# Four low weight parts: a negated copy on ScalarE and an adding transfer instead of a subtract on VectorE

## The chip, the cores and the metric

The kernel runs on one core of a Trainium2 chip. The metric is the device time of one execution in microseconds (us). Three runs of the kernel before gave 973.69, 974.58 and 974.63 us; their median is 974.58.

In the profile PE is the engine of the matrix products, DVE the vector engine, ACT the scalar engine, POOL the GpSimd engine and SP the engine that here issues nearly all transfers.

## The reference

```
mag = sqrt(a_re^2 + a_im^2);  a = (a_re + i a_im) * min(mag, 0.999) / (mag + 1e-6)
for t in range(768):                       # per batch (4) and head (8), state is 48 x 48, complex
    S = a[t] * S + k[t] (outer) v[t]
    y[t] = q[t] @ real(S)
x = y as 3072 tokens x 384
x = (h - tanh(h)) @ w_out1   with h = x @ w_in1      # 384 -> 2048 -> 384
x = (relu(h)^2) @ w_out2     with h = x @ w_in2
```

The weights come as 64-bit floats. The products have to be nearly as good as float32.

## The kernel before

The recurrence is cut into six chunks of 128 time steps for each of four batch entries, which makes 24 units (`unit`). Tokens are worked in six groups of 512; the two feed-forward layers are worked in 16 blocks m of 128 hidden columns for each group. A block is nine products into `h` (`g1`), an activation (`act_parts`), and nine products into three accumulators `acc` (`g2`), two blocks later. There are nine because every operand is held as a high part, rounded to the format fp32r that PE multiplies at full pace, and a low part, the rest: for each of three slices of the contraction, high times high, high times low and low times high are added up.

The weights of a block are 128 x 768 values, `w_in` and `w_out` side by side. They are loaded as 64-bit words into `st` (768 KB, two buffers), joined to float32 by three DVE instructions into `cv` (two buffers, tag "cv", `conv_do`, lines 214 to 239), and split by `conv_split` (line 270) with `split_w` (line 276): ACT writes the high part `wh`, DVE subtracts it from `cv` and writes the low part `wl`. A `cv` buffer is free again when both have read it, and the block after next then writes it. `wh` and `wl` have a place of their own for each m in `wpool`. The places of m = 4 to 15 are first used by tiles of the units 1 to 3 (`early`), all of which are done with when these weights are written.

The order of the work: a list START starts the first units and blocks of weights, then `block_step(t)` is called for each block; t = 0 and 1 are the two halves of m = 0, t = 2 is m = 1, and so on to t = 16, which is m = 15. At block t, `conv_upto` brings the joining of weights up to `JOINS` blocks ahead. So the split of m = 4 is issued at the block of m = 2, that of m = 5 at m = 3, those of m = 6 and 7 at m = 4, and that of m = 14 at m = 11. On PE and SP each engine's order is then as written (`Turn`, and `chain`); on DVE and ACT it is pinned from t = 17 and t = 15 on, and before that, in all of the stretch that the change touches, the framework's list scheduler chooses among what is ready by its own durations. Each engine works its queue in order: an instruction whose wait is not over holds up all behind it.

POOL writes constants at the start and then has nothing to do until it splits tokens for the second layer. All transfers but one, an output at the very end, go out on SP's queue.

Of the kernel before, what the change touches and what calls it, by code (L numbers as in the profile page):

```python
# [12 lines left out]
F32 = mybir.dt.float32  # L13
# [4 lines left out]
ALU = mybir.AluOpType  # L18
# [18 lines left out]
1x 0pU 2s0 2m0 0st 3e0 3s0 2e1 4sq J 4ln 1st 3s1 3pU 3m0 2s1 2m1 3st 3m1 2px 3px 2pU 2st B 2x 3x  # L37
"""
AHEAD = (1, 1, 1, 2, 2, 3, 4, 5, 5, 6, 7, 8, 8, 8, 9, 9, 10, 11, 11, 11, 12, 13, 13, 15, 15, 15, 16, 16)
JOINS = (4, 2, 3, 3, 4, 3, 2, 2, 2, 2, 3, 4, 3, 2, 2, 3, 4)  # L40


@with_exitstack
def kernel(
# [9 lines left out]
    nc = tc.nc  # L54
# [47 lines left out]
    def clear_strips():  # L102
# [11 lines left out]
        out=maskab[:, 0], in_=maskab[:, 0], compare_op=ALU.is_ge, fill=0.0, base=0,  # L114
        pattern=[[1, P]], channel_multiplier=-1,
    )
    for g in range(4):
        m = maskab[32 * g:32 * g + 32, 1]
        nc.gpsimd.affine_select(
            out=m, in_=m, compare_op=ALU.is_ge, fill=0.0, base=-32 * (3 - g),  # L120
# [6 lines left out]
        out=past, in_=past, compare_op=ALU.is_ge, fill=0.0, base=-1,  # L127
# [41 lines left out]
    act_e = Turn(nc.scalar, "act")  # L169
# [44 lines left out]
    def conv_do(layer, m):  # L214
        st = stg.pop((layer, m))
        lo, hi = words(st)
        if layer == 0:
            t = spool.tile([P, n2], I32, tag="cv", name=f"cv{layer}_{m}", bufs=2)
        else:
            t = cpool[0].tile([P, n2], I32, tag="jw", name=f"jw{m}", bufs=2)  # L220
        tf = t.bitcast(F32)
        with ExitStack() as es:
            if (layer, m) == (0, 1):
                es.enter_context(tc.issue_after(chain["gate"]))
            dve.tensor_scalar(
                t, hi, 3, 0x3FFFFFFF, op0=ALU.logical_shift_left, op1=ALU.bitwise_and
            )
        yield
        dve.scalar_tensor_tensor(
            t, lo, 29, t, op0=ALU.logical_shift_right, op1=ALU.bitwise_or  # L230
        )
        yield
        dve.scalar_tensor_tensor(
            t, hi, -0x40000000, t, op0=ALU.bitwise_and, op1=ALU.bitwise_or
        )
        if layer == 0 and 0 < m < NM - 1:
            conv_split(layer, m, tf)
        else:
            joined[m] = tf
# [30 lines left out]
    def conv_split(layer, m, tf):  # L270
        wh = wpool.tile([P, n2], F32R, tag=f"wh{m}", name=f"wh{layer}_{m}")
        wl = wpool.tile([P, n2], F32R, tag=f"wl{m}", name=f"wl{layer}_{m}")
        split_w(wh, wl, tf)
        wts[layer, m] = (wh, wl)

    def split_w(wh, wl, tf):
        act_e.copy(wh, tf)
        dve.tensor_tensor(wl, tf, wh.bitcast(F32), op=ALU.subtract)
# [755 lines left out]
    def conv_upto(k):  # L1034
        while cdone[0] < k:
            conv_tick()
# [20 lines left out]
    s_first = 3 - (NST - 1)  # L1057
    pos = AHEAD
    assert len(pos) == NM - s_first
# [59 lines left out]
    def block_step(t):  # L1119
# [3 lines left out]
        if t < NB0:  # L1123
            conv_upto(min(NM, blocks[t][2] + JOINS[t]))
            steps = ahead[t]
# [5 lines left out]
        if t < NB:  # L1131
# [8 lines left out]
            if t == NB0 - 2:  # L1140
                conv_split(0, NM - 1, joined.pop(NM - 1))
# [34 lines left out]
        if t >= NATT + LAG:  # L1176
            for _ in range(2):
                if cdone[0] < len(cq):
                    conv_tick()
            m2 = cur["split"]  # L1180
            if m2 in joined and t >= NATT + LAG + m2:
                conv_split(1, m2, joined.pop(m2))
                cur["split"] += 1
# [122 lines left out]
```

## Time and profile before

| | us |
|---|---|
| median of three runs | 974.58 |
| the profiled execution | 973.18 |
| its span, first to last instruction | 971.1 |
| PE busy | 950.1 (98%) |
| ACT busy | 635.2 (65%) |
| DVE busy | 540.7 (56%) |
| POOL busy | 19.5 (2%) |

The page gives busy times of the whole span; its line of 40 slices shows that DVE and ACT are at nine or ten tenths in the first five or six slices (some 24 us each) and far below that later, and that PE's granted clock is 0.9 or more in every slice. A busy PE is not a PE at its full pace, because products are pipelined: a product of 512 columns is shown as 0.39 us, while the next starts after 0.23 us.

### The profile page before, as it was taken

The numbers are of one execution on the slowest core, as the hardware profiler recorded it, in microseconds if no ns is written. First come the engines' busy times: TensorE is split into PE (matmuls) and PEld (weight loads), VectorE is DVE, ScalarE is ACT, GpSimd is POOL, SyncE is SP. The second block draws the span as 40 slices with busy tenths as digits, with TensorE's granted clock in tenths as the row PEclk, the third lists the DMA queues.
The fourth block names the chain that finished last, engine by engine and source line by source line (L and its number), as shares of the span: only waits on it lengthen the run. The fifth ranks groups of instructions, "written<-read, shape, count | busy, mean of one in ns | idle before, by whom it ended". The sixth has DMA issues, their size and how long they took to land.

```text
span 971.1 us, 18373 instructions
## 1 busy us (share of the span) xinstructions
PE 950.1 (98%) x7437; PEld 786.2 (81%) x7437; DVE 540.7 (56%) x902; ACT 635.2 (65%) x1110; POOL 19.5 (2%) x43
## 2 busy tenths in 40 slices
PE   5999999999999999999999999999999999999997
PEld 2888788888888888888888888888888888888886
DVE  7999987666666666665548993132322322322111
ACT  8879978777777777786534455465666665555442
POOL 2000000000000000000000010000000000000000
PEclk9999999999999999999999999999999999999999
DMA  8345413222322232221136552063444353330001
GB/s 315 131 148 165 151 45 92 59 58 64 101 68 70 63 92 64 69 75 42 58 126 224 176 169 79 1 195 104 163 143 140 93 176 113 130 97 31 33 1 34
DMA packets 53481, 100.99 MB, mean 104 GB/s; under 512 B 19712, under 2 KB 29200, under 8 KB 53392
## 3 DMA queue, kind: packets, MB, share of 16 engines
q1 hardware_dynamic: 53248, 99.65, 32.4%
q8 instruction: 59, 0.97, 0.4%
q14 instruction: 30, 0.25, 0.1%
q10 hardware_dynamic: 144, 0.13, 0.0%
HBM read 87.08 MB, written 9.46 MB: 99 GB/s over the span
## 4 chain that ended last, share of the span: by engine, by line
PE 89%; ACT 5%; DVE 5%; DMA 1%; issue 1%; ACTq 0%
PE h L161 39%; PE acc L161 38%; PE px L161 3%; PE strips L161 2%; PE pk L161 1%; PE pq L161 1%; ACT ab L161 1%; PE pU L161 1%; DVE cv L161 1%; ACT L161 1%; PE pu L161 1%; PE sc L161 1%; PE pc L161 1%; ACT fg L161 1%; ACT ee L161 1%
## 5 line engine op out<-in xcount | busy, mean ns | idle before, releaser
L161 DVE TENSOR_TENSOR gl<-t,gh 128x512 fp32r<-128x512 f32 (+1 forms) x193 | 132.2, 685 | 215.4 <-ACT gh L161 215.1
L161 ACT ACTIVATE t<-h 128x512 f32<-128x512 f32 (+1 forms) x193 | 114.6, 594 | 194.0 <-PE h L161 191.4
L161 PE MATMUL acc<-gh,wh 128*128 128x512 f32 (+1 forms) x579 | 229.3, 396 | 0.0
L161 PE MATMUL h<-xh,wh 128*128 128x512 f32 (+1 forms) x579 | 228.0, 394 | 0.6 <-DVE t L161 0.4
L161 PE MATMUL h<-xh,wl 128*128 128x512 f32 (+1 forms) x579 | 225.1, 389 | 0.0
L161 PE MATMUL acc<-gl,wh 128*128 128x512 f32 (+1 forms) x579 | 225.0, 389 | 0.0
L161 PE MATMUL acc<-gh,wl 128*128 128x512 f32 (+1 forms) x579 | 224.8, 388 | 0.0
L161 PE MATMUL h<-xl,wh 128*128 128x512 f32 (+1 forms) x579 | 224.0, 390 | 0.0
L161 ACT CAST gh<-t 128x512 fp32r<-128x512 f32 (+1 forms) x191 | 118.0, 618 | 87.0 <-PE acc L161 46.2
L161 PEld LDWEIGHTS h<-xh,wh 128*128 128x128 f32 x579 | 108.7, 188 | 26.6 <-issue 3.2
L161 PEld LDWEIGHTS h<-xh,wl 128*128 128x128 f32 x579 | 108.7, 188 | 22.7
L161 PEld LDWEIGHTS acc<-gh,wl 128*128 128x128 f32 x579 | 108.7, 188 | 22.6
L161 PEld LDWEIGHTS acc<-gl,wh 128*128 128x128 f32 x579 | 108.9, 188 | 21.9 <-DVE gl L161 0.2
L161 PEld LDWEIGHTS acc<-gh,wh 128*128 128x128 f32 x579 | 108.8, 188 | 21.6
L161 PEld LDWEIGHTS h<-xl,wh 128*128 128x128 f32 x579 | 108.7, 188 | 21.1
L161 DVE TENSOR_TENSOR t<-h,t 128x512 f32<-128x512 f32 (+1 forms) x97 | 65.8, 679 | 59.8 <-ACT t L161 59.7
L161 ACT ACT_TABLE_LOAD x63 | 80.8, 1283 | 1.7 <-PEq L1288 0.8
L161 ACT ACTIVATE t<-t 128x512 f32<-128x512 f32 x96 | 60.3, 628 | 1.6
L161 DVE TENSOR_TENSOR wmin<-wmin,cz 128x768 bf16<-128x768 bf16 x32 | 17.8, 557 | 57.4 <-ACT cz L161 57.4
L161 DVE TENSOR_TENSOR wm<-strips,maskab 128x512 f32<-128x512 f32 x32 | 21.8, 690 | 29.1 <-PE strips L161 29.1
L161 DVE SCALAR_TENSOR_TENSOR jw<-st,jw 128x768 int32<-128x768 int32 x32 | 30.4, 950 | 0.2
L161 DVE SCALAR_TENSOR_TENSOR cv<-st,cv 128x768 int32<-128x768 int32 x32 | 30.4, 949 | 0.2
(141 smaller groups left out, 977.7 us busy)
## 6 DMA issues: line engine op xcount, KB each, us to landing
st<-in_w_dram SPq DMA_DIRECT2D x32, 768.0 KB
sr<-in_w_dram SPq DMA_DIRECT2D x32, 768.0 KB
ri<-in_ri_dram SPq DMA_DIRECT2D x24, 384.0 KB
qk<-in_qk_dram SPq DMA_DIRECT2D x24, 384.0 KB
vz<-in_v_dram SPq DMA_DIRECT2D x16, 384.0 KB
x2d<-x2t SPq DMA_DIRECT2D x18, 256.0 KB
xf<-x2d SPq DMA_DIRECT2D x6, 768.0 KB
ss<-in_ri_dram SPq DMA_DIRECT2D x12, 384.0 KB
```

The source lines that it names most:

```text
L161: r = op(*a, **kw)
```

## The change

For m = 4, 5, 6 and 14 of the first layer, the low part is made in another way: ACT writes minus the high part into `wl`, and a transfer from POOL's queue adds `cv` to it in place. The other twelve blocks of the first layer and all of the second keep the subtract on DVE.

```diff
+BY_DMA = (4, 5, 6, 14)
 JOINS = (4, 2, 3, 3, 4, 3, 2, 2, 2, 2, 3, 4, 3, 2, 2, 3, 4)
...
         wh = wpool.tile([P, n2], F32R, tag=f"wh{m}", name=f"wh{layer}_{m}")
         wl = wpool.tile([P, n2], F32R, tag=f"wl{m}", name=f"wl{layer}_{m}")
-        split_w(wh, wl, tf)
+        if layer == 0 and m in BY_DMA:
+            act_e.copy(wh, tf)
+            act_e.mul(wl, wh.bitcast(F32), -1.0)
+            nc.gpsimd.dma_start(out=wl, in_=tf, accum_op=ALU.add)
+        else:
+            split_w(wh, wl, tf)
         wts[layer, m] = (wh, wl)
```

## Rows read from the trace of the kernel before

**Rows 1.** Busy time by stretch: stretch, length, PE, PEld, DVE, ACT, POOL, clock, DMA, GB/s.
```profile
50.00:60.00 10.00, 10.00 (x116) 8.78 (x105) 9.84 (x18) 6.34 (x15) 0.00 (x0) 1.00 0.42 151
60.00:70.00 10.00, 9.81 (x45) 7.78 (x44) 9.93 (x16) 9.03 (x15) 0.00 (x0) 1.00 0.49 158
...
520.00:960.00 440.00, 440.00 (x1943) 364.06 (x1942) 164.91 (x242) 243.59 (x428) 11.73 (x15) 1.00 0.33 107
```

**Rows 2.** PE's longest group of waits, 50 to 150 us: who, whom, us, times, longest.
```profile
PE pk L161 <- DVE kn L161: 1.0, 2, 0.7
```

**Rows 3.** Writes of `wh` up to 140 us: count, ns least/median/most, first, last.
```profile
L161 ACT CAST wh<-cv x16: 818/832/890, 18.3 to 131.1; 128x768 fp32r<-128x768 f32 x16
```

**Rows 4.** POOL in order of time, its first instruction after the start: start us, us, instruction, wait.
```profile
504.84 0.62 POOL L361 TENSOR_SCALAR xh<-xf 128x512 fp32r<-128x512 f32 x1 [498.41 <-DVE gl L161]
```

**Rows 5.** SP in order of time, the load of 384 KB before DVE's wait.
```profile
133.78 0.35 SPq L161 DMA_DIRECT2D qk<-in_qk_dram  x1
```

**Rows 6.** Busy time by stretch, columns as in the first group, while a load of `st` runs.
```profile
51.00:52.00 1.00, 1.00 (x11) 0.95 (x9) 1.00 (x3) 0.69 (x3) 0.00 (x0) 1.00 1.00 418
```

**Rows 7.** DVE in order of time, 49 to 69 us, around weights and activations.
```profile
49.71 0.95 DVE L161 TENSOR_TENSOR wl<-cv,wh 128x768 fp32r<-128x768 f32 x1
...
53.58 0.55 DVE L161 TENSOR_SCALAR cv<-st 128x768 int32<-128x768 int32 x1
...
54.79 0.96 DVE L161 TENSOR_TENSOR wl<-cv,wh 128x768 fp32r<-128x768 f32 x1 [0.16 <-ACT wh L161]
55.67 0.42 DVE L161 TENSOR_TENSOR gl<-t,gh 128x256 fp32r<-128x256 f32 x1
...
59.61 0.55 DVE L161 TENSOR_SCALAR cv<-st 128x768 int32<-128x768 int32 x1
60.08 0.95 DVE L161 TENSOR_TENSOR wl<-cv,wh 128x768 fp32r<-128x768 f32 x1
...
66.68 0.55 DVE L161 TENSOR_SCALAR cv<-st 128x768 int32<-128x768 int32 x1
...
68.14 0.68 DVE L161 TENSOR_TENSOR t<-h,t 128x512 f32<-128x512 f32 x1
```

**Rows 8.** PE in order of time, places that wait for what the change moves.
```profile
56.14 0.39 PE L161 MATMUL acc<-gl,wh 128*128 128x256 f32 x1
...
68.88 0.50 PE L161 MATMUL h<-xh,wh 128*128 128x512 f32 x1 [0.19 <-DVE t L161]
...
100.79 0.39 PE L161 MATMUL h<-xh,wl 128*128 128x512 f32 x1
101.27 0.61 PE L161 MATMUL pk<-ident,kn 128*96 128x128 f32 x4
...
132.12 0.40 PE L161 MATMUL h<-xh,wl 128*128 128x512 f32 x1
...
133.90 0.61 PE L161 MATMUL pk<-ident,kn 128*96 128x128 f32 x4 [0.69 <-DVE kn L161]
```

**Rows 9.** ACT in order of time, 50 to 67 us.
```profile
50.28 0.49 ACT L161 ACTIVATE xh<-px 128x384 fp32r<-128x384 f32 x1 [0.69 <-PE px L161]
...
59.86 0.59 ACT L161 ACTIVATE t<-h 128x512 f32<-128x512 f32 x1
...
66.94 0.60 ACT L161 ACTIVATE t<-h 128x512 f32<-128x512 f32 x1
```

**Rows 10.** DVE in order of time, 82 to 137 us, its waits.
```profile
82.77 0.69 DVE L161 TENSOR_TENSOR gl<-t,gh 128x512 fp32r<-128x512 f32 x1 [1.03 <-ACT gh L161]
...
124.60 0.95 DVE L161 TENSOR_TENSOR wl<-cv,wh 128x768 fp32r<-128x768 f32 x1
...
131.93 0.96 DVE L161 TENSOR_TENSOR wl<-cv,wh 128x768 fp32r<-128x768 f32 x1 [0.86 <-ACT wh L161]
...
136.88 0.96 DVE L161 TENSOR_TENSOR qk<-qk,ee 128x768 f32<-128x768 f32 x1 [0.79 <-DMA qk<-in_qk_dram]
```

**Rows 11.** ACT in order of time, its longest wait from 123 to 132 us.
```profile
126.23 0.62 ACT L161 CAST gh<-t 128x512 fp32r<-128x512 f32 x1 [1.63 <-DVE t L161]
```

## Prediction

> **What bounds the kernel now.** I read the page's busy times first, then busy time by stretch, then who waited for whom on PE, and last PE, DVE and ACT in order of time between 49 and 137 us, where the four weights are split.
>
> From 520 us on PE starts 1943 products in 440 us, 0.226 us each, without a wait [rows 1]. That is its full pace, so the time is what PE has to do plus what it stands still. Between 50 and 60 us PE is already never idle, and from 60 to 70 us it is idle for 0.19 us [rows 1]. The reader is to see two things in these rows: PE is the bound as soon as the blocks begin at 51 us, and DVE (9.84 and 9.93 of 10) is as full as PE there, ACT first much less (6.34), then nearly so (9.03). From 50 to 150 us PE stands 1.0 us before transposes, for DVE's `kn` [rows 2], and 0.19 for its `t` [rows 8]. Beside that there are stops too short for that view: a product starts 0.23 us after the one before it, but the transposes at 101.27 start 0.48 after the product at 100.79 [rows 8], 0.25 late; I count four such places of 0.1 to 0.3, some 0.9 us. So however much DVE is relieved, some 2.1 us are all that PE has to give there.
>
> **The change, part by part.** Four subtracts of 0.95 us go from DVE [rows 7, 10]. Its next instruction starts before such a one has ended (at 55.67 behind the one at 54.79, 0.88 later [rows 7]), so DVE gets 4 x 0.88 = 3.5 us. ACT gets four negations. The trace has no copy with a factor of this size; the nearest is the copy that writes `wh`, 128 x 768 in 0.832 us [rows 3], and I take 0.75 for its share of the queue, 3.0 us in all. From below it could be a DVE instruction of one input, 0.55 [rows 7], from above a subtract, 0.95.
>
> POOL gets four transfers to issue. Behind them stands nothing until 504.84 us [rows 4]. SP's queue is not touched, but for loads of `st` that DVE's joining releases.
>
> *How long the adding transfer takes* is the unknown. It moves 384 KB within the chip's memory, reads both operands, and is issued by POOL, which issued none before. The nearest row is a load of 384 KB: issued at 133.78, DVE goes on with it at 136.88, 3.1 us [rows 5, 10]. The lower end is the data alone at the best rate that I find, 393 KB at 418 GB/s = 0.94 us [rows 6], with 0.35 for an issue [rows 5]: 1.3 us. The upper end is twice the load, 6.2, and on top an issue on POOL as long as its one instruction of 128 x 512, 0.62 [rows 4]: 6.8 us. I take 4.5 us, the load and half of it again for the second operand; for m = 4 a load of `st` fills the transfer engines until 52 [rows 6], so no less there.
>
> *Who waits for it.* PE needs `wl` late. The split of m = 14 was at 124.60 and PE first reads it at 132.12 [rows 8, 10]: with the negation in the subtract's place (done by some 124.85), a transfer of up to 7.3 us is hidden, beyond my upper end. The blocks 4, 5 and 6 are read some 14 us after their splits; they are hidden with more room. What comes earlier is the `cv` buffer, which is not free until the transfer has read it. The first joining instruction of m + 2 writes it, and on DVE everything behind that instruction waits too:
> m = 4: negation in the subtract's place, done at 49.71 + 0.75 = 50.46 (the wait of 0.69 before 50.28 [rows 9] hides it), m = 6 begins at 53.58 [rows 7]: free up to 3.1 us.
> m = 5: done at 54.79 + 0.75 = 55.54, m = 7 begins at 59.61: free up to 4.1 us.
> m = 6: done at 60.08 + 0.75 = 60.83, m = 8 begins at 66.68: free up to 5.9 us. After m = 14 nobody takes the buffer soon.
>
> *First stop.* At 4.5 us m = 6 begins at 54.96 instead of 53.58, 1.38 later. Behind it in DVE's order stand a bias of the decay, the subtract of m = 5, now gone (0.88), and the `gl` of the first half block at 55.67; that is then at 56.17, done at 56.59, and PE, which used it at 56.14 [rows 7, 8], at some 56.6 less the 0.05 us that it had to spare: some 0.4 us lost. m = 7 is 0.5 late and no more; after the third subtract DVE is about 0.4 ahead of before.
>
> *ACT.* From 59.86 to 66.94 ACT goes through eleven instructions without a wait, the last being the tanh of m = 3 [rows 9], and DVE's `t` behind it at 68.14 ends the 0.19 us that PE stands still before 68.88 [rows 7, 8]. The negation of m = 6 falls in there, so the tanh ends at 68.25 instead of 67.5, `t` is at 68.3 instead of 68.14, and PE goes on 0.17 later. Of the first stop's 0.4, 0.2 hide in that wait, since ACT and not PE sets it: together 0.4. That DVE is ahead ends soon: at 82.77 it stands 1.03 us for ACT's `gh` [rows 10], so the waits of PE for `kn` behind that are not moved by m = 4 to 6.
>
> *m = 14.* ACT's wait of 1.63 us before 126.23 [rows 11] hides the negation. DVE has 0.88 us less ahead of it, but already stands 0.86 before the subtract of m = 15, for ACT's `wh` [rows 10], and behind that comes the `kn` for which PE stands 0.69 before 133.90 [rows 8]. If ACT's order stays, nothing is won; if `wh` of m = 15 moves up by what DVE's joining is earlier, up to 0.69. I take 0.4 as won.
>
> Sum: 0.4 lost, 0.4 won, nothing. The profiled execution took 973.18 (its span 971.1 and 2.1 around it), and so would one of the changed kernel; the median of the runs stands 1.4 above it, which makes **974.6 us**: no change.
>
> A rule that speaks against the change is in the Trainium skill, SBUF — State Buffer, section "SBUF: two separate sides": a transfer issued from GpSimd has its descriptors written by GpSimd, which is locked out while VectorE runs a copy-like instruction in its two-port mode, and one that took 0.62 us alone took 3.1 us beside such a copy. DVE's one-input joining instruction takes 0.55 us for as much as 0.95 with two inputs [rows 7], so that mode seems to run here; no run of before issues from POOL. By the rule each transfer would be up to 2.5 us longer, an estimate, and the sum that of the slow rival.
>
> **The rivals.**
> *The buffer holds DVE up (slower).* One mechanism: the transfer lands 6.8 us after the negation, and DVE stands before m = 6 and m = 7. For it: DVE has no idle time there [rows 1] and runs in order. Against it: 6.8 is twice the load that the trace shows, and the scheduler may put other work ahead of the joining. m = 6 begins at 57.26, 3.68 late; with the next subtract gone `gl` is 2.8 late, and PE loses as much, less the 0.19 at 68.88. m = 7 begins at 62.3, 2.7 late as well, so nothing is added. 974.6 + 2.6 = 977.2. Slower by over 0.2% it is from about 6.1 us on. The rule above would give this.
> *DVE was the bound (faster).* What DVE is ahead reaches all that PE stands for it, 1.0 and 0.19 and the short stops, 0.9 [rows 2, 8]. For it: DVE is at 9.9 of 10 [rows 1]. Against it: DVE itself waits for ACT at 82.77 and at 131.93 [rows 10]. 974.6 - 2.1 = 972.5.
> *ACT becomes the bound.* Two of the three early negations find no wait of ACT that hides them, and their 1.5 us reach PE through `t`. For it: 9.03 of 10 from 60 us on. Against it: 6.34 before [rows 1], where two of the three are. 974.6 + 1.5 = 976.1.
> *It does nothing.* Everything is hidden and the scheduler's order stays: 974.6.
>
> **How the numbers follow.** What a measurement tells from no change is 0.2%, 1.95 us. My forecast 0.44, it does nothing 0.07, ACT as the bound 0.1: within. Slow rival 0.2, fast rival 0.19. The order of DVE and ACT is the scheduler's in this stretch and can shift each case by a microsecond; so some of the forecast's chance lies outside the 0.2%, and some of the rivals' within, about as much. Faster by over 0.2%: 0.19; within: 0.61; slower: 0.20. The range reaches from the fast rival to the slow one, 972.3 to 977.0.
>
> **What would show it.** In the profile after: DVE's first joining instruction of m = 6 with a wait for a transfer of about 1 us or none (over 2: the slow rival); no wait of PE for a transfer before the products of m = 14 (one would break the 7.3 us bound); ACT without a wait between 60 and 67 us and PE's stop near 69 longer by some 0.2; PE's stop near 134 the same or gone. The prediction is wrong if the adding transfer takes over 6 us, or if PE's waits for DVE from 50 to 150 us come to over 2.5 us.

## The result, and the profile after

| | before | after |
|---|---|---|
| median, us (lowest to highest) | 973.75 (973.38 to 974.63) | 980.82 (978.43 to 982.45) |
| ratio, 95% interval | 1 | 1.0069 (1.0054 to 1.0085) |
| the profiled execution, us | 973.18 | 982.45 |
| its span, us | 971.1 | 980.6 |

The change costs 0.69%, some 7 us. The forecast was 974.6, no change, with a range of 972.3 to 977.0, and the time lies above it. The profiled execution of after is its slowest one, so its parts add up to 9.5 us of span and not to 7.

Busy time by stretch (after; columns as in [rows 1]). From 520 us on PE starts nearly as many products as before (1939, 1943), but between 50 and 60 us it is idle for 2.6 us, where it had been full, and DVE, which had been busy for 9.84 of 10, is busy for half of that:

```profile
50.00:60.00 10.00, 7.39 (x101) 6.41 (x94) 5.16 (x9) 5.11 (x12) 1.87 (x2) 0.97 0.90 231
60.00:70.00 10.00, 10.00 (x46) 8.52 (x45) 9.23 (x16) 9.10 (x15) 0.84 (x1) 0.86 0.70 199
520.00:960.00 440.00, 439.51 (x1939) 363.41 (x1938) 168.56 (x245) 241.63 (x426) 12.21 (x15) 1.00 0.34 112
```

PE's waits from 50 to 150 us (after), beside [rows 2]. The 2.6 us stand in one wait for `gl`:

```profile
PE acc L162 <- DVE gl L162: 2.6, 1, 2.6
PE pk L162 <- DVE kn L162: 1.3, 2, 0.7
```

DVE and PE in order of time (after), beside [rows 7, 8]. DVE comes to the first joining instruction of m = 6 at 53.55, as early as before, and stands 4.55 us for the transfer of m = 4. Right behind it in its queue is the `gl` that PE needs; PE's two products of one group, 0.14 us apart in before (56.00, 56.14), start 2.89 apart:

```profile
53.13 0.42 DVE L162 TENSOR_TENSOR t<-h,t 128x256 f32<-128x256 f32 x1 [0.25 <-ACT t L162]
58.11 0.56 DVE L162 TENSOR_SCALAR cv<-st 128x768 int32<-128x768 int32 x1 [4.55 <-DMA wl<-cv]
58.59 0.42 DVE L162 TENSOR_TENSOR gl<-t,gh 128x256 fp32r<-128x256 f32 x1
```

```profile
56.17 0.28 PE L162 MATMUL acc<-gh,wh 128*128 128x256 f32 x1
59.06 0.39 PE L162 MATMUL acc<-gl,wh 128*128 128x256 f32 x1 [2.61 <-DVE gl L162]
```

POOL's transfers in order of time (after). The first is issued at 50.95 and lets DVE go on at 58.11, 7.2 us later. While it is on its way a load of `st` (issued at 51.98) and the second transfer (54.14) come on to the same engines:

```profile
50.95 1.00 POOL L277 DMA_DIRECT2D wl<-cv  x1 [44.49 <-DVE cv L162]
54.14 0.87 POOL L277 DMA_DIRECT2D wl<-cv  x1 [2.18 <-ACT gh L162]
63.59 0.84 POOL L277 DMA_DIRECT2D wl<-cv  x1 [8.58 <-ACT wl L162]
129.82 0.86 POOL L277 DMA_DIRECT2D wl<-cv  x1 [65.39 <-ACT wl L162]
```

The same view in steps of 1 us (after; the last two columns are the share of the transfer engines and GB/s). From 54 to 55 the engines are full and move no more than 104 GB/s; with the load of `st`, from 55 on, it is 326:

```profile
54.00:55.00 1.00, 1.00 (x7) 0.86 (x6) 0.00 (x0) 1.00 (x3) 0.86 (x1) 1.00 0.96 104
55.00:56.00 1.00, 1.00 (x6) 0.80 (x5) 0.00 (x0) 0.14 (x1) 0.01 (x1) 1.00 1.02 326
```

Behind its stop PE is slower for 3 us. In these windows (after) the third column from the right, the granted clock, falls to 0.50, which is 1.2 instead of 2.4 GHz; in before it is 1.00 throughout [rows 1]. Products start 0.43 us apart (60.73, 61.16) instead of 0.23:

```profile
59.00:60.00 1.00, 0.94 (x5) 0.94 (x6) 1.00 (x3) 0.00 (x0) 0.00 (x0) 0.67 0.22 49
60.00:61.00 1.00, 1.00 (x6) 1.00 (x5) 1.00 (x4) 0.76 (x2) 0.00 (x0) 0.50 0.06 12
61.00:62.00 1.00, 1.00 (x3) 0.72 (x3) 1.00 (x3) 0.56 (x2) 0.00 (x0) 0.50 0.05 9
62.00:63.00 1.00, 1.00 (x4) 0.84 (x3) 0.96 (x3) 0.97 (x2) 0.00 (x0) 0.63 0.63 104
```

```profile
60.73 0.63 PE L162 MATMUL h<-xh,wh 128*128 128x512 f32 x1
61.16 0.63 PE L162 MATMUL h<-xl,wh 128*128 128x512 f32 x1
```

What does not show in any wait of PE is the end. The last product starts at 965.26 in before and at 972.49 in after:

```profile
965.26 0.28 PE L161 MATMUL strips<-gh,wl 128*128 128x256 f32 x1
```

```profile
972.49 0.28 PE L162 MATMUL strips<-gh,wl 128*128 128x256 f32 x1
```

From there to the end of the span it is 5.84 us in before and 8.11 in after. SP's waits from 960 us on, for its own closing instructions, show most of the 2.3 us (before first, then after):

```profile
SPq L1241 <- SPq L1241: 2.7, 1, 2.7
```

```profile
SPq L1247 <- SPq L1247: 4.8, 2, 2.8
```

So the span's 9.5 us are 7.2 on PE and 2.3 behind it. In this execution the stop and the clock are 2.8 (2.89 less the usual distance) and some 1.7 (what the granted clock of the four windows from 59 to 63 us falls short of 1.00, added up) of the 7.2. How large the first stop is differs between executions of the same order, though, and e13 below shows that the 7 us do not hang on it.

### The profile page after: what moved, and what is told of

Same layout as the page of the kernel before. It is cut to its first block, busy times and chain, and to the rows that moved or that the text cites. A ratio compares the mean times of both kernels' runs of the same rounds, so it can differ in the third digit from the quotient of the medians.

```text
span 980.6 us, 18398 instructions
## 1 busy us (share of the span) xinstructions
PE 951.4 (97%) x7437; PEld 787.4 (80%) x7437; DVE 538.7 (55%) x898; ACT 637.6 (65%) x1114; POOL 23.6 (2%) x47
## 4 chain that ended last, share of the span: by engine, by line
PE 78%; DVE 7%; ACT 2%; DMA 1%; issue 1%; ACTq 0%; DVEq 0%
PE h L162 34%; PE acc L162 34%; PE px L162 3%; DVE jw L162 3%; PE strips L162 2%; DVE wl L162 1%; PE pq L162 1%; PE pk L162 1%; DMA st<-in_w_dram 1%; DVE gl L162 1%; PE pU L162 1%; DVE t L162 1%; ACT L162 1%; PE pu L162 1%; PE pc L162 1%
## 5 line engine op out<-in xcount | busy, mean ns | idle before, releaser
L367 POOL TENSOR_SCALAR xh<-xf 128x512 fp32r<-128x512 f32 x18 | 14.4, 826 | 690.8 <-DVE gl L162 380.6
```

Source lines behind the costliest of these rows:

```text
L367: nc.gpsimd.tensor_scalar(xh[:, kk], xf[:, kk], 1.0, 0.0, op0=ALU.mult, op1=ALU.add)
```

## The experiments

The theories, in the order in which they came up. A: the `cv` buffer, held by the transfer, is what costs. B: ACT's negations cost. C: the transfers themselves cost, by crowding the loads. D: with four subtracts fewer on DVE, the list scheduler chooses another order for DVE, ACT and SP, and that order is what costs. E and F, on the end: the length of SP's program, or the transfers on POOL's queue.

| kernel | median, us | ratio to before, 95% | last product | from there to the end |
|---|---|---|---|---|
| after | 980.82 | 1.0069 (1.0054 to 1.0085) | 972.49 | 8.11 |
| e1 places for m = 4, 5 | 980.33 | 1.0066 (1.0049 to 1.0082) | 969.19 | 7.91 |
| e2 only m = 14 | 975.86 | 1.0018 (1.0008 to 1.0028) | 966.11 | 7.49 |
| e3 only m = 4 | 975.49 | 1.0016 (1.0006 to 1.0026) | 966.67 | 5.83 |
| e4 no transfer, DVE adds | 974.06 | 0.9999 (0.9989 to 1.0009) | 966.08 | 6.22 |
| e5 places for m = 4, 5, 6 | 977.89 | 1.0039 (1.0026 to 1.0053) | 967.92 | 7.98 |
| e6 transfers beside the subtracts | 976.14 | 1.0020 (1.0010 to 1.0030) | 966.19 | 8.31 |
| e7 POOL subtracts | 980.32 | 1.0063 (1.0047 to 1.0080) | 972.46 | 5.74 |
| e8 only m = 4, 5 | 978.89 | 1.0052 (1.0033 to 1.0070) | 969.07 | 7.93 |
| e9 after, order of before | 977.14 | 1.0030 (1.0018 to 1.0042) | 967.42 | 7.68 |
| e10 e9 with places | 976.81 | 1.0026 (1.0014 to 1.0037) | 966.97 | 7.93 |
| e11 e7, order of before | 976.18 | 1.0021 (1.0012 to 1.0030) | 968.38 | 5.62 |
| e12 before, longer branch | 975.55 | 1.0017 (1.0008 to 1.0026) | 966.21 | 7.39 |
| e13 after, shorter branch | 977.95 | 1.0044 (1.0030 to 1.0058) | 971.48 | 5.92 |
| e14 before, shorter branch | 973.60 | 0.9998 (0.9989 to 1.0007) | 966.34 | 5.86 |
| e15 e10 with shorter branch | 974.52 | 1.0006 (0.9996 to 1.0015) | 966.70 | 6.00 |

The last two columns are from the one profiled execution of each. e12 and e14 execute the same instructions as before, and their last product is at 966.2 and 966.3, so a single profile is good to about 1 us here, and before's was an early one. e3's was early too: 974.80 us, where its median is 975.49.

**e1, e5: the buffer.** The joined weights of some m get places of their own in `wpool`, which units 1 to 3 have done with, so no joining waits for their transfer.

```diff
+OWN = {4: "wl15", 5: "wh15"}            # e5: and 6: "wh14"
...
+            if m in OWN:
+                t = wpool.tile([P, n2], F32, tag=OWN[m], name=f"cv{layer}_{m}").bitcast(I32)
+            else:
                 t = spool.tile([P, n2], I32, tag="cv", name=f"cv{layer}_{m}", bufs=2)
```

> The changed kernel, but the joined weights of m = 4 and 5 lie in places of their own (those of the later wl and wh of m = 15), so that no later block waits for their transfers. Theory A, the held buffer (in the profile of the changed kernel DVE stands 4.55 us at the first joining instruction of m = 6, PE 2.6 us behind it, and PE's granted clock is 0.5 for 3.4 us after): DVE's wait, PE's stop near 56 us and the low clock are gone, 973 to 976 us. Theory B, ACT's four negations and the order that the scheduler makes with them: nothing changes, 978 to 982. Theory C, what transfers from POOL cost beside that (loads of st slowed, SP's wait at the very end, 2.0 us longer): PE's stop goes, but 976 to 978 stay.

In e1 the wait before m = 6 and the fall of the clock are gone, but the time is that of after. DVE waits elsewhere, for the transfer of m = 6 and for loads of `st`, and PE stands 2.8 us for `ri`, which stands behind the joining of m = 8 in DVE's queue. DVE's and PE's waits from 50 to 150 us (e1):

```profile
DVE cv L163 <- DMA wl<-cv: 1.9, 1, 1.9
DVE cv L163 <- DMA st<-in_w_dram: 1.7, 2, 1.5
```

```profile
PE pu L163 <- DVE ri L163: 2.8, 1, 2.8
```

> All four transfers stay, but the joined weights of m = 4, 5 and 6 now lie in places of their own, so no joining instruction of m = 6, 7 or 8 can wait for a transfer. Theory A (what costs is the buffer that the transfer holds): DVE's wait for the transfer, which with places for m = 4 and 5 alone came back as 1.9 us at m = 8, is gone altogether, and the time falls to 974 to 976. Theory C (what costs is the traffic itself: transfers on POOL's queue and the loads of st get in each other's way, and the end of the program is longer): DVE waits for st instead, and the time stays at 979 to 981.

With no hold left at all (e5), 3.5 of the 7 us remain, between the two expectations; PE's longest wait is 1.3 us, for the same `ri`. A alone does not explain the result. Both kernels have orders of their own on DVE, different from before's and after's, so what they save is not the price of the hold alone.

**e2, e3: one transfer.**

```diff
-BY_DMA = (4, 5, 6, 14)
+BY_DMA = (14,)                          # e3: (4,)
```

> Only m = 14 is split by negation and transfer; the order on DVE is that of before but for the one subtract. Theory A: no buffer is held, as nothing takes that buffer soon; 973 to 975 us. Theory B: a quarter of the loss, 975 to 976. Theory C: if one transfer from POOL is enough for the longer end, 2 us, 975.5 to 976.5; else as A.

> Only m = 4 is split by negation and transfer. Theory A: most of the loss is here, since this transfer held m = 6 up: DVE stands some 3 to 5 us at the first joining instruction of m = 6 and PE's clock may fall; 976.5 to 980 us. If a second transfer in flight made the first one late, the wait is shorter, 1 to 2 us, and 974.5 to 976. Theory B: a quarter of the loss, 975 to 976.

Both times fit more than one theory: e2's 975.86 lies in the ranges of B and C and above A's, e3's 975.49 in B's and in A's second one. Alone, the transfer of m = 14 lands 4.1 us after its issue and that of m = 4 5.0 us. DVE's wait for the transfer in e3, all there is of it from 45 to 150 us:

```profile
DVE cv L162 <- DMA wl<-cv: 0.5, 1, 0.5
```

In e2 DVE's order is before's but for the missing subtract, PE's last product is where e12's and e14's are, and the whole loss is in the end. So m = 14's relief of DVE gains nothing on PE, whose two waits for `kn` are before's, 1.0 us.

**e4: ACT alone.** ACT writes the negation, DVE adds.

```diff
-            nc.gpsimd.dma_start(out=wl, in_=tf, accum_op=ALU.add)
+            dve.tensor_tensor(wl, tf, wl.bitcast(F32), op=ALU.add)
```

> For the same four weights ACT writes minus the high part, but DVE adds the joined weight to it, in place of the transfer: ACT's part alone, DVE as full as before. Theory A: no buffer is held, 973.5 to 976 us. Theory B: ACT's 3.1 us and the new order make the loss, 977 to 982. Theory C: as A, with no longer end.

Within 0.1% of before, with the four negations in ACT's queue, so they do not make the 7 us, and B falls. Here the scheduler put a `t` of ACT ahead of the negation of m = 6, and PE's stop near 69 us is 0.43 us, where it had been 0.19 [rows 8]. The negations (busy time and mean ns of one, e4):

```profile
L162 ACT ACTIVATE wl<-wh 128x768 fp32r<-128x768 f32 x4 | 3.4, 845 | 0.0
```

**e6: the traffic.** The subtracts stay on DVE; ACT's negations and POOL's four transfers run beside them into places that nobody reads.

```diff
-            act_e.copy(wh, tf)
-            act_e.mul(wl, wh.bitcast(F32), -1.0)
-            nc.gpsimd.dma_start(out=wl, in_=tf, accum_op=ALU.add)
+            split_w(wh, wl, tf)
+            side = wpool.tile([P, n2], F32R, tag=SIDE[m], name=f"side{m}")
+            act_e.mul(side, wh.bitcast(F32), -1.0)
+            nc.gpsimd.dma_start(out=side, in_=wh, accum_op=ALU.add)
```

> The four subtracts stay on DVE. ACT writes the negations into four other places, and POOL's adding transfers (same size, same points) add wh there: nobody reads the result and no cv buffer is held by a transfer. Left over is what the traffic and ACT's four instructions cost. Theory A: 974 to 975.5, as with ACT's negations alone. Theory C: 978 to 981, with loads of st that come late and a longer end.

PE's last product is at 966.19, as in e12 and e14: with the order kept, all four transfers and all four negations cost PE nothing. The 1.7 us are the end (8.31), and the time lies between the two expectations. C falls for PE. PE's longest group of waits from 50 to 150 us is before's [rows 2] (e6):

```profile
PE pk L163 <- DVE kn L163: 1.0, 2, 0.7
```

**e7, e8.** e7 takes the subtracts off DVE without any transfer; e8 keeps two of the four transfers.

```diff
-            act_e.mul(wl, wh.bitcast(F32), -1.0)
-            nc.gpsimd.dma_start(out=wl, in_=tf, accum_op=ALU.add)
+            nc.gpsimd.tensor_tensor(wl, tf, wh.bitcast(F32), op=ALU.subtract)
```

> The four subtracts are done by POOL's own instruction, without negation and without transfer. DVE is relieved of the same 3.5 us as by the change. From POOL's row of 0.62 us for 128 x 512 with one input I estimate 0.9 to 1.9 us for 128 x 768 with two; the buffer is then free before m + 2 begins. Theory A and C alike: no wait of DVE for POOL, 972.5 to 974.5; what it wins is what DVE's relief is worth, at most 2.1 by the prediction. Over 976 would mean that another cost lies in taking the subtract off DVE (the order that the scheduler then chooses, or POOL and DVE in each other's way).

This one turned the study: no transfer, no negation, the same relief of DVE, and 980.3 us, with the last product as late as after's. PE's waits from 50 to 150 us (e7) are many and short, none over 1.3:

```profile
PE pk L162 <- DVE kn L162: 1.4, 3, 0.7
PE pu L162 <- issue: 1.3, 1, 1.3
PE acc L162 <- DVE gl L162: 1.0, 1, 1.0
...
```

> Only m = 4 and 5 by transfer, everything else as in the kernel after. m = 4 alone cost 1.4 us. Theory A: two transfers in flight make the first one land late, DVE stands over 3 us before m = 6 and PE stops 2.8 us as in the kernel after, with the fall of the clock behind it: 978 to 979. Theory C in proportion to the number of transfers: two of four, 976.5 to 977.5.

978.9 is what A expected, but not by its mechanism: PE's wait for `gl` is 0.5 us, not 2.8. The kernels fall in two groups. Where DVE's order up to 140 us is nearly before's (e2, e4, e6), PE loses nothing; in e3, in between, 0.5; where much of it is moved (after, e1, e5, e7, e8), PE loses 1.7 to 6.3 us against e12 and e14. That is theory D.

**e9, e10, e11: the order of before.** The four engines' orders are read from the kernel before and fixed by edges that only tell what is issued after what; the four subtracts are missing, a negation stands right behind its `wh`.

```diff
+    for e, order in ORDER.items():       # creation numbers in the order of before
+        seq = [SEEN[e][int(k)] for k in order.split() if SEEN[e][int(k)] is not None]
...
+        for a, o in zip(seq, seq[1:]):
+            tc.add_manual_dep(o, a.name, mybir.DependencyInfo(
+                mybir.DependencyClass.NoSync, mybir.DependencyReason.DATA), reason="order")
```

> The kernel after, but PE, DVE, ACT and SP get the order of the kernel before by edges that only fix the order of issue (the four subtracts missing, each negation right behind its wh). New theory D (with the subtracts gone the scheduler chooses another order for DVE and ACT, and that order costs most): what is left is the hold of the buffers and the longer end, 975.5 to 978, and the stops of PE behind 65 us are as before. Theory A/C (hold and traffic): nothing changes, 980 to 981.

The order alone takes 980.82 to 977.14, and the last product from 972.49 to 967.42. DVE and PE in order of time (e9). The hold is still there, 2.25 us, but behind the joining stands what stood there in before, and PE loses 0.58 there and not 2.6; the granted clock stays at 1.00:

```profile
55.50 0.56 DVE L290 TENSOR_SCALAR cv<-st 128x768 int32<-128x768 int32 x1 [2.25 <-DMA wl<-cv]
...
56.46 0.42 DVE L290 TENSOR_TENSOR gl<-t,gh 128x256 fp32r<-128x256 f32 x1
```

```profile
56.93 0.39 PE L290 MATMUL acc<-gl,wh 128*128 128x256 f32 x1 [0.58 <-DVE gl L290]
```

A second stop stands behind it. The negation of m = 6 right behind its `wh` puts off ACT's next `t`, DVE waits for that (e9), and near 70 us PE stands 1.0 us for DVE's `t`, where it had been 0.19 [rows 8]. It is the same in e10, where nothing is held (DVE in order of time, e9; PE's waits from 50 to 150 us, e10), and in e15:

```profile
62.14 0.69 DVE L290 TENSOR_TENSOR t<-h,t 128x512 f32<-128x512 f32 x1 [1.19 <-ACT t L290]
```

```profile
PE h L291 <- DVE t L291: 1.0, 1, 1.0
```

> The same order, and the joined weights of m = 4, 5 and 6 in places of their own, so that no joining waits for a transfer. Theory D: PE's stops as before or fewer, left over are traffic and the end: 974 to 976. Theory A/C: as with the places alone, 977 to 979.

Taking the hold away as well gives 0.3 us more (976.81), which the intervals do not tell from nothing. It stayed above its expected 974 to 976, since the end (7.93) is not touched.

> The four subtracts on POOL by its own instruction (about 2 us each), no transfer, and the order of before on PE, DVE, ACT and SP. With the scheduler's own order it took 980.3. Theory D: 972.5 to 974.5, PE's last product within 1 us of before or earlier; what it is below 974.4 is the worth of DVE's 3.5 us. Theory A/C: POOL's subtracts or the missing DVE work cost by themselves, 977 to 981.

The same edges take the kernel with POOL's subtracts from 980.32 to 976.18, above D's 974.5 and below the other theories' 977. So the order is worth about 4 us with transfers (3.7) and without (4.1): D is shown. Which engine's order carries it is not separated, since the edges fix all four. What e11 still loses it does not lose to the end (5.62) but on PE, and its trace tells a part: while POOL subtracts, DVE is slow. POOL and DVE in order of time (e11):

```profile
49.76 1.82 POOL L406 TENSOR_TENSOR wl<-cv,wh 128x768 fp32r<-128x768 f32 x1 [43.33 <-ACT wh L290]
55.57 1.83 POOL L406 TENSOR_TENSOR wl<-cv,wh 128x768 fp32r<-128x768 f32 x1 [3.99 <-ACT wh L290]
```

```profile
49.91 2.49 DVE L290 SCALAR_TENSOR_TENSOR cv<-st,cv 128x768 int32<-128x768 int32 x1
...
55.83 1.86 DVE L290 TENSOR_TENSOR gl<-t,gh 128x256 fp32r<-128x256 f32 x1 [0.36 <-ACT gh L290]
```

**e12 to e15: the end.** The table's last column has two levels: 5.6 to 6.2 us, and 7.4 to 8.3. SP's program is 938 instructions long in before, 944 in e3 (short end), 946 in e2 and e8 and 953 in after (long end). Against before, after, before and e10, in this order, these four change only the branch for unusual inputs, which is not taken.

```diff
# e12, in the branch that is not taken
+            pad = cp.tile([1, 12, D], F32, name="g_pad")
+            for i in range(12):
+                nc.sync.dma_start(pad[:, i], v[0, i:i + 1, 0, :D])
# e13, e14, e15, twice in it
-                    for b in range(B):
+                    for b in range(1):
```

> The kernel before, with twelve loads more in the branch that isn't taken: SP's program has 954 instructions instead of 938, as many as that of the kernel after (953), and executes the same ones. Theory E (the longer end is SP's program crossing a block of 8 KB that has to be loaded at the end; the runs so far had it with 946 or more instructions on SP and not with 944 or fewer): SP stands 1.5 to 2 us near the end, 975.7 to 976.7. Theory F (the end is longer because of the transfers on POOL's queue): no change, 974 to 974.6.

> The kernel after, with the loads of three of four batch entries left out in the branch that isn't taken: SP's program has 919 instructions instead of 953. Theory E: the end is as short as before's, 1.7 to 2.1 us less than the kernel after, 978 to 979.5. Theory F: as the kernel after, 980 to 981.5.

> The kernel before with the same loads left out in the branch that isn't taken: 904 instructions on SP. A control: with theory E or F no change, 973.8 to 974.6; a lower time would mean that leaving these out gives something beside the end.

> The change with before's order, own places for the joined weights of m = 4, 5 and 6, and the shorter branch (919 instructions on SP). Theories D and E together: the order, the hold and the end are gone, 974.5 to 975.2, left over is PE's last product 1.7 us later than before's in the profile with that order. With E wrong: 976.5 to 977.

e13 executes what after executes, in the same order on every engine, and so is a second execution of it. The first stop is small in it: the hold is 2.41 us instead of 4.55, PE loses 0.47, the clock stays at 1.00 there. DVE and PE in order of time (e13):

```profile
55.98 0.56 DVE L162 TENSOR_SCALAR cv<-st 128x768 int32<-128x768 int32 x1 [2.41 <-DMA wl<-cv]
56.46 0.42 DVE L162 TENSOR_TENSOR gl<-t,gh 128x256 fp32r<-128x256 f32 x1
...
65.69 0.56 DVE L162 TENSOR_SCALAR cv<-st 128x768 int32<-128x768 int32 x1 [0.85 <-DMA wl<-cv]
...
67.04 0.95 DVE L162 SCALAR_TENSOR_TENSOR cv<-st,cv 128x768 int32<-128x768 int32 x1
...
68.78 0.55 DVE L162 TENSOR_TENSOR ri<-ri,ab 128x384 f32<-128x384 f32 x1
...
71.18 0.54 DVE L162 SCALAR_TENSOR_TENSOR ri<-cr,ri 1x384 f32<-1x384 f32 x1
```

```profile
56.93 0.39 PE L162 MATMUL acc<-gl,wh 128*128 128x256 f32 x1 [0.47 <-DVE gl L162]
...
71.78 1.33 PE L162 MATMUL pu<-ri,maskt 128*128 128x384 f32 x2 [2.04 <-DVE ri L162]
```

What was not lost there is lost 15 us later: PE stands 2.04 us for `ri`, and behind that stop the granted clock is 0.50 from 73 to 75 us. DVE writes `ri` in more than one step; the last, at 71.18, lets PE go on, the first shown is at 68.78. In DVE's new order the joining of m = 8, two instructions of it and its wait for the transfer of m = 6, stands ahead of the first of these. In before that one comes first, at 65.75, the joining of m = 8 at 66.68 [rows 7], and the last step at 68.75, 2.4 us earlier than in e13:

```profile
65.75 0.55 DVE L161 TENSOR_TENSOR ri<-ri,ab 128x384 f32<-128x384 f32 x1
...
68.75 0.54 DVE L161 SCALAR_TENSOR_TENSOR ri<-cr,ri 1x384 f32<-1x384 f32 x1
```

By the `pu` of a later unit the two executions of after's order are equally late, 5.2 and 5.0 us behind before (before, after, e13):

```profile
113.45 0.91 PE L161 MATMUL pu<-ri,maskt 128*128 128x384 f32 x2
```

```profile
118.67 0.81 PE L162 MATMUL pu<-ri,maskt 128*128 128x384 f32 x2
```

```profile
118.42 0.81 PE L162 MATMUL pu<-ri,maskt 128*128 128x384 f32 x2
```

As to the end: without a transfer, and with the same instructions executed (e12), a longer program makes before slower by 0.17%, with the end at 7.39; e12's 975.55 lies just under what E expected, as e13's and e14's times do. With all transfers kept, a shorter one takes the end of after back to 5.92 and its ratio from 1.0069 to 1.0044, and that of e10 from 1.0026 to 1.0006. F falls. So the length of SP's program makes the end longer, executed or not. That the time is the loading of code is not shown. In after one packet of an instruction queue, and nothing else, is moved from 975.8 to 979.2 us. But so it is in e14, whose end is short, from 969.9 to 972. And SP's waits do not place the time in every kernel: in e12, e2 and e8, all with a long end, the wait for its own closing instructions is one, of 2.8, 2.7 and 2.9 us, as in before.

By the ratios the 0.69% are: the order 0.39 (after to e9), the hold 0.04 (e9 to e10), the end 0.20 (e10 to e15; 0.25 from after to e13), and 0.06 that cannot be told from nothing. By the intervals each of these differences is uncertain by 0.15 to 0.2 of a percent, so the order and the end are clear of noise and the hold is not. No kernel here beats before; e15, with the transfers but without the new order, the hold and the longer end, is level with it.

## Why the prediction was wrong

**What bounds the kernel: right.** PE is the bound from 51 us on, and what the traces name of the loss before the end is stops of PE and its slower clock. Also right is that the relief of DVE is worth little: e15, which has all of it in the order of before, is not faster, and PE's waits for `kn` stay at 1.0 us.

**ACT: right in size, too low in what hangs on it.** A negation takes the 0.75 us of ACT's queue that were forecast (the next instruction starts at 50.55 behind the one at 49.80, after; 0.845 as the trace shows one, e4). The sum had PE's stop near 69 us grow from 0.19 by 0.17; with ACT's `t` ahead of the negation (e4) it is 0.43, near that, but with the negation right behind its `wh` (e9, e10, e15) it is 1.0. The text followed the tanh at 66.94; in e9 the one at 59.86 in before [rows 9] stands behind the negation too, and DVE waits 1.19 us for it. In after this stop does not show. ACT is also full for longer than the part ahead of the prediction says: at seven to nine tenths in the first 18 of the 40 slices of before, not only in the first six.

**The step that failed: the sum was made in the order of before.** "Behind it in DVE's order stand a bias of the decay, the subtract of m = 5, now gone (0.88), and the `gl`": in after, `gl` stands right behind the joining. The text knew that the order is the scheduler's and let it "shift each case by a microsecond"; it measured 3.7 (980.82 to 977.14), and was the largest term; the one place of it that the traces name is `ri` behind the joining of m = 8. In e9, where the order is the one of the sum, the step comes out as worked, with a somewhat longer transfer: m = 6 begins at 55.50 (forecast 54.96), `gl` at 56.46 (56.17), and PE uses it at 56.93, 0.8 later than in before (0.4).

**The transfer's time: under-sized by less than it seemed.** Forecast were 4.5 us from the end of the negation, which is 50.65 in after, to DVE's go. With before's order it was 5.0 (50.46 to 55.50, e9), with after's 5.3 in one execution (55.98, e13) and 7.5 in the other (58.11, after), beyond the upper end of 6.8. What made it late there is not the rule of the Trainium skill (SBUF — State Buffer, section "SBUF: two separate sides") that GpSimd is kept from writing descriptors while VectorE runs in its two-port mode: from the issue at 50.95 to 53.55 DVE ran two-input instructions, none of the one-input kind that the prediction took for that mode, then it stood still to 58.11, and each issue took POOL 0.84 to 1.00 us. None of the four issues had such an instruction beside it, so the rule itself is not tested. Beside the transfer were a load of `st` and the transfer of m = 5; why the engines moved only 104 GB/s there, and what differs between the two executions, stays open.

**The slow rival** had the mechanism of after's first stop (PE loses 2.6 us for `gl`), in the execution that happened to be profiled. Both signs that the prediction set for being wrong showed there: a transfer of over 6 us (7.5) and over 2.5 us of waits of PE for DVE from 50 to 150 us (4.7). It is not the cause of the 7 us: e13 lost 0.47 there and is as late at the end of the stretch. Without that second execution the trace of after alone would have made the rival the explanation.

**m = 14:** the 0.4 won is not there. In e2 the last product is no earlier than in e12 and e14, and PE's longest wait for `kn` is before's 0.7.

**The end: not in the sum.** "Its span 971.1 and 2.1 around it" was carried over as a constant; 15 more instructions on SP made it about 2 us longer.

## What to carry to other kernels

In a stretch that a list scheduler orders, taking an instruction away is a change of everything behind it: price it in the new order, or fix the old one first and then judge the edit, as e9 and e11 do. Before a transfer replaces an engine's work, ask what it keeps occupied and what stands right behind the next writer; alone its time tells little of its time in company. When a change adds instructions, compare the time behind the last product too, and check it with a kernel that is only longer.

## What the runs showed of the hardware

The same subtract on POOL (1.8 us) stretched DVE's two-input instructions beside it from 0.95 to 2.49 and from 0.42 to 1.86 us (e11). PE's granted clock fell to 0.50 right behind a stop of 2.6 us and came back some 3 us later (after), and did so behind the 2.0 us of e13; behind the 2.8 us of e1 and e9's 0.58 it stayed at 1.00. With 938 instructions in SP's program the time behind the last product was 5.84 us (before) and with 944 5.83 (e3); with 946 it was 7.49 (e2) and with 953 8.11 (after), and in e12, where 16 of 954 are only added and not executed, 7.39.
